# One exponential per head, and the check of the bounds put together at the end, in a top-k attention kernel

## The chip, the core and the metric

The kernel runs on one core of one Trainium2 chip. A core has five engines that each work through a queue of their own in order: TensorE (PE in the profile; PEld is its weight load), VectorE (DVE), ScalarE (ACT), GpSimd (POOL) and SyncE (SP), which here only starts transfers. They wait for one another through semaphores. The metric is the time of one execution in microseconds on the device: 827.2 us before the change, the median of three runs (826.03 to 827.62).

## What is computed

The reference is attention that keeps the 32 largest scores of each row, and behind it a mixture-of-depths block:

```python
# q, k, v: (8 batches, 8 heads, 576 tokens, 64), float32
scores = scale * np.matmul(q, k.transpose(0, 1, 3, 2))
kth = np.partition(scores, -top_k, axis=-1)[..., -top_k:-top_k + 1]   # top_k = 32
scores = np.where(scores >= kth, scores, -1000000000.0)
attn = np.exp(scores - max)            # max over each row
attn = attn / (sum of attn + 1e-09)
x = np.matmul(attn, v)                 # then (8, 576, 512), the heads side by side
# per batch b:
s = x[b] @ w_gate                      # 576 numbers
top_idx = the 128 tokens with the largest s
h = np.maximum(x[b, top_idx] @ w1, 0)  # w1: 512 x 1024
out[b, top_idx] = x[b, top_idx] + sigmoid(s)[:, None] * (h @ w2)
```

## The kernel before, in words

**Units.** The work is cut into 144 units `(b, t, g)`, 18 to a batch: a block of 128 query rows (the last block of a batch has 64, so it holds four heads instead of two) by two heads. A unit has two score tiles of 128 x 576, index `i` = 0 and 1; below they are called its two heads.

**What a unit goes through.** `multiply` computes the scores in PSUM and `keep` copies them out on ACT (`sc`). `find_bound` on DVE finds a lower bound of the 32nd largest score from the eight largest of each of seven parts. `what_is_below` marks on ACT which scores lie under the bound (`sides`) and counts them into `seen`, and on POOL forms `y`; `kth_of` on DVE takes the exact 32nd largest from `y` into `next8`. `mask_of` writes `less`, a 0/1 mask or a positive distance of what is too small, for one head on ACT and for the other on POOL. `weigh` transposes the scores on PE into `ptr` with, after each transposed block, a matmul that adds a hugely negative number where `less` is set (`turn`), does the same for the remaining 64 + 64 columns of both heads in the bank of `av` (`turn_last`), and then applies the exponential on ACT: one ACTIVATE over both heads, 1024 numbers in each partition, into `pT`, and one for `last`. `values` multiplies `pT` and `last` by v, `keep_values` copies the result to `xs`, and once per four units DVE and POOL normalise it.

**The order.** The loop at L1094 issues, in iteration n, work of different units: the exponential and the values of unit n-4, the mask of n-3, the 32nd largest of n-2, `what_is_below` of n-1, the bound of n, and the scores of n+1. All engines keep the order of the program (`InOrder`, L37), so this order is the order of each queue. Within an iteration, ACT has: exponentials of n-4 (L1124), mask of n-3, what the list `late` holds (`flush`, L1127), copies of transposed q and k, the copy of the scores (L1140), the copy of the values, then the two `sides`. PE has: the transposes and masks of n-4, the scores of n+1, the values of n-4, and a piece of the mixture of an earlier batch (its two matrix products are spread over the units of the next batch but one, at the places in `mix_at`).

**The check.** The shortcut through the bound is only right for ordinary inputs, so the kernel collects evidence and at the end decides whether to run a general version. For each batch, in the mask of its last unit (L1091), `keep_least` (L1073) takes the 36 bounds of each partition, tests with one bit operation on DVE whether a bound's mantissa is the wrong one (`low`), and reduces bounds, 32nd largest scores and `low` to one number each in `least`. For the last batch that is at L1255, in the tail. There the evidence is put together on DVE into `sure` (L1256 to L1278), and `count_unsure` multiplies `sure` by ones on PE (L1285).

**The tail.** After the loop, the last four units are finished in an order of their own (L1214 to L1252), `other_room` lending the scores' PSUM space to every second unit, and `closing` (L746) does the mixture of the last batch: gather of the chosen rows, four transposes, `xeT` copied by ACT, 64 matmuls with w1, 16 with w2, and the scatter. `closing` is a generator: what stands between two of its `yield`s goes into the queues between other work. The check stands at L1255 to L1281, after the step of `closing` that ends with `flush()` (L828), in which ACT gets `gy<-y_ps,g` of the batch before; and `count_unsure` stands ahead of the matmuls with w1 in PE's queue.

**PSUM.** It has eight banks: four for the scores (`ps`), two for `ptr`, one for `av`, one for the rest.

Of the kernel before, what the change touches and what calls it, by code (L numbers as in the profile page):

```python
# [26 lines left out]
LEAST = 1.0e-16 * SMALLER  # L27
# [4 lines left out]
J = 4  # L32
# [16 lines left out]
def kernel(  # L49
# [11 lines left out]
    nc = tc.nc  # L61
    P = nc.NUM_PARTITIONS
    B, H, S, D = q.shape
# [5 lines left out]
    R = S - JP  # L69
# [4 lines left out]
    scale = 1.0 / float(D) ** 0.5 / SMALLER  # L74
# [55 lines left out]

    NS = B * 2 * (J * NHP + NHP // 2)
    seen = const.tile([P, NS], FP32, name="seen")
    least = const.tile([P, 3, B], FP32, name="least")
    sums = const.tile([P, B * NT, H], FP32, name="sums")
    nc.gpsimd.memset(sums, 1.0)

# [50 lines left out]
    def flush():  # L187
        while late:
            late.pop(0)()
# [119 lines left out]
                    )  # L309

    def turn_pair(rows, hp, copy=None):
        tr = ps_tr.tile([P, 2, J, P], FP32, name="ptr")
        for w in range(2):
            rows.turn(2 * hp + w, tr[:, w, :, :])
        for w in range(2):
            rows.keep(2 * hp + w, tr[:, w, :, :], copy=copy)

    def turn_all_last(rows, copy=None):
        tr = ps_misc.tile([P, 2, 2, P], FP32, name="tr", tag="misc")
# [149 lines left out]
    def turn_some(tr, z, less):  # L469

        pe.transpose(tr, z, ident)
        if less is not None:
            pe.matmul(
                tr, less, out_of_reach, start=False, stop=True, skip_group_check=True
            )

    def room_to_turn():
        return ps_tr.tile([P, 2, J, P], FP32, name="ptr"), ps_av.tile(
            [P, 512], FP32, name="av"
        )  # L480

    def turn(z, tr, less=None):

        for i in range(2):
            for c in range(J):
                at = slice(c * P + i * R, (c + 1) * P + i * R)
                turn_some(
                    tr[:, i, c, :], z[:, i, at], None if less is None else less[:, i, at]
                )

    def turn_last(z, av, less=None):
# [11 lines left out]
    def values(t, g, pT, last, av, vs):  # L503

        vt, vpair = vs
        for i, heads in enumerate(heads_of(t, g)):
            for c in range(J):
                for r in (0, R):
                    h = heads[-1 if r else 0][0]
                    pe.matmul(
                        av[r : r + R, i * DE : (i + 1) * DE],
                        pT[:, i, c, r : r + R],
                        vt[:, h, c, :],
                        start=(c == 0 and i == 0),  # L520
                        stop=False,
                        skip_group_check=True,
                    )
# [222 lines left out]
    def closing(b, pg, between):  # L746
# [7 lines left out]
        pick = modpool.tile([P, NT, CAP], BF16, name="pick")  # L754

        def spread(t0, t1):
            tr = ps_tr.tile([P, 2, J, P], FP32, name="ptr")
            n = R if t0 == J else P
            for t in range(t0, t1):
                pe.transpose(  # L760
                    tr[:, 0, t - t0, 0:n],
                    gate[0:n, t : t + 1].to_broadcast([n, P]),
                    ident[0:n, 0:n],
                )
            act.copy(
                out=gate_row[:, t0 * P : (t1 - 1) * P + n].rearrange(
                    "p (t i) -> p t i", i=n
                ),
                in_=tr[:, 0, 0 : t1 - t0, 0:n],
            )  # L770

        def count(t, among, rank):
# [59 lines left out]
        dve.reciprocal(out=g, in_=g)  # L832

        xeT = modpool.tile([P, NDC, CAP], FP32, name="xeT")
        ps = ps_tr.tile([P, 2, J, P], FP32, name="ptr")[:, 0, :, :]
        for dc in range(NDC):
            pe.transpose(ps[:, dc, :], xe[:, dc * P : (dc + 1) * P], ident)
        act.copy(out=xeT, in_=ps)
# [2 lines left out]
        for f0 in range(0, NFC, 2):  # L841
            h_ps = (
                lambda: room_for_scores()[:, 0, 0, :],
                lambda: ps_av.tile([P, 512], FP32, name="av"),
                lambda: ps_misc.tile([P, 512], FP32, name="h_ps", tag="misc"),
                lambda: ps_tr.tile([P, 2, J, P], FP32, name="ptr")[:, 0, :, :].rearrange(
                    "p c i -> p (c i)"
                ),
            )[f0 // 2 % 4]()
# [186 lines left out]
    def weigh(sc, tr, av, less):  # L1036

        turn(sc, tr, less)
        tr_last = turn_last(sc, av, less)
        pT = ptpool.tile([P, 2, J, P], FP32, name="pT")  # L1040
        last = ptpool.tile([P, P], FP32, name="last")

        def exp():
            act.activation(pT, tr, AF.Exp, scale=scale)
            act.activation(last, tr_last, AF.Exp, scale=scale)

        return pT, last, exp
# [23 lines left out]
        find_kth(ys.pop(n), next8s[b][:, i, :, :])  # L1071

    def keep_least(b, bound, kth):  # L1073
        low = stats.tile([P, per_batch, 2], I32, name="low", bufs=1)
        dve.tensor_scalar(
            out=low,
            in0=bound.bitcast(I32),
            scalar1=(1 << 23) - 1,
            scalar2=1,
            op0=ALU.bitwise_and,  # L1080
            op1=ALU.bitwise_xor,
        )
        for w, of in enumerate((bound, kth, low)):
            dve.tensor_reduce(
                out=least[:, w, b : b + 1], in_=of, axis=mybir.AxisListType.XY, op=ALU.min
            )

    def mask_of(n, on=None):
        b, i = divmod(n, per_batch)
# [97 lines left out]

    def other_room():
        ps = room_for_scores()
        return ps[:, 0, :, :].rearrange("p u (c i) -> p u c i", c=J), ps[:, 1, 0, :]  # L1190

    x, pg = of_batch[B - 1]
    between = mixtures[B - 2]
# [59 lines left out]


    keep_least(B - 1, bounds.pop(B - 1)[:, :, :, 7], next8s.pop(B - 1)[:, :, :, 7])  # L1255
    sure = stats.tile([P, 1], FP32, name="sure")  # L1256
    dve.memset(sure, 1.0)
    for what, op, than, limit in (
        (least[:, 0, :], ALU.min, ALU.is_gt, LEAST),
        (least[:, 1, :], ALU.min, ALU.is_gt, LEAST),  # L1260
        (least[:, 2, :], ALU.min, ALU.is_gt, 0.5),
        (seen, ALU.max, ALU.is_lt, float(MIDDLE)),
        (seen, ALU.min, ALU.is_gt, float(MIDDLE - 16)),
        (sums.rearrange("p t h -> p (t h)"), ALU.min, ALU.is_gt, FEWEST),
        (sums.rearrange("p t h -> p (t h)"), ALU.max, ALU.is_lt, MOST),
    ):
# [62 lines left out]
    def general(b, row0):  # L1329
        def of(a):  # L1330
            return a[bass.ds(b, 1)].rearrange("o a s d -> (o a) s d")

        kT, qT, vs = room_for_qkv(0)
        rows = Rows(of(k), of(q), kT, qT)
        turn_all_last(rows)
        for hp in range(NHP):
            turn_pair(rows, hp)
        load_v(of(v), vs)
        x = xpool.tile([P, NT, HD], FP32, name="x")
        pg = gates_of[0]  # L1340
        for t in range(NT):
            xs = xpool.tile([P, H, DE], FP32, name="xs")
            for g in range(groups(t)):
                ps = room_for_scores()
                multiply(t, g, kT, qT, ps)
                p = general_weights(keep(ps))
                tr, av = room_to_turn()
                turn(p, tr)
                pT = ptpool.tile([P, 2, J, P], FP32, name="pT")
                last = ptpool.tile([P, P], FP32, name="last")  # L1350
                nc.scalar.copy(out=pT, in_=tr)
# [12 lines left out]
        flush_all()  # L1364
# [40 lines left out]
```

## Time and profile before

The profile is of one execution of its own:

| | before |
|---|---|
| median of three runs | 827.2 us |
| the profiled execution, as timed | 828.44 us |
| its span, first to last instruction | 826.1 us |
| its mean granted TensorE clock | 0.990 |
| busy: DVE, PE | 787.2 us, 777.0 us |
| busy: ACT, POOL | 730.7 us, 715.4 us |

So 2.3 us of the profiled execution lie outside its span, and it is 1.2 us over the median. In the lines of a profile, `out<-in` gives the tiles that an instruction writes and reads, `x` the number of instructions that a line stands for, and a bracket the idle time ahead of it and what ended that. Nearly all instructions are recorded under L45, the helper that issues them in order, so they are told apart by their tiles.

### The profile page before, as it was taken

What the parts mean: (1) busy time and instruction counts of PE and PEld (TensorE: products, weight loads), DVE (VectorE), ACT (ScalarE), POOL (GpSimd) and SP (SyncE); (2) the same over time, 40 slices, a digit from 0 to 9 for tenths busy, and PEclk for the clock granted to TensorE, in tenths of its full rate; (3) what the DMA queues carried; (4) which work ended last, traced back from release to release, by engine and by line L of the source; (5) the groups of instructions that cost most, each with busy time, mean ns of one, the idle gap of its engine ahead of it and who ended that gap; (6) DMA issues with size and microseconds to landing.
All of it is one profiled execution on the core that took longest, in us unless ns stands there. A gap on an engine that the chain in (4) does not pass through costs nothing. (4 is left out here: it accounts for less than half of the span.)

```text
span 826.1 us, 28252 instructions
## 1 busy us (share of the span) xinstructions
PE 777.0 (94%) x10143; PEld 596.5 (72%) x10143; DVE 787.2 (95%) x4651; ACT 730.7 (88%) x1557; POOL 715.4 (87%) x722
## 2 busy tenths in 40 slices
PE   6888888888999999999999999999999999999976
PEld 5566666666887778877787777877787777767744
DVE  7899999999999999999999999999999999999960
ACT  4799999999999999999999999999999999879831
POOL 3799999999899999999899999999999998899831
PEclk9699999999999999999999999999999999999999
DMA  7931111521141221521223221512215102101021
GB/s 170 283 86 40 28 66 28 105 53 27 60 92 36 53 40 59 112 47 34 79 47 86 53 40 60 104 23 54 40 59 112 28 15 66 23 12 18 2 71 30
DMA packets 122133, 50.38 MB, mean 61 GB/s; under 512 B 116417, under 2 KB 116417, under 8 KB 120961
## 3 DMA queue, kind: packets, MB, share of 16 engines
q1 hardware_dynamic: 118672, 43.91, 22.0%
q0 software_dynamic: 1728, 4.20, 2.8%
q8 instruction: 82, 1.34, 0.8%
q14 instruction: 67, 0.54, 0.3%
q10 hardware_dynamic: 1584, 0.39, 0.2%
HBM read 36.93 MB, written 11.55 MB: 59 GB/s over the span
## 5 line engine op out<-in xcount | busy, mean ns | idle before, releaser
L45 POOL TENSOR_TENSOR y<-sc,sides 128x576 f32<-128x576 f32 x288 | 365.1, 1289 | 57.0 <-ACT sides L45 54.3
L45 DVE MAX8 cand<-sc 128x8 f32<-128x82 f32 (+1 forms) x2016 | 314.0, 228 | 2.7 <-ACT sc L45 2.7
L45 POOL TENSOR_SCALAR less<-sc,next 128x576 bf16<-128x576 f32 x135 | 232.5, 1722 | 12.9 <-DVE next L45 10.0
L45 PE MATMUL ptr<-out_of_reach,less 128*128 128x128 bf16 x1136 | 205.3, 220 | 19.5 <-POOL less L45 19.4
L45 ACT ACTIVATE sides<-sc,bound 128x576 bf16<-128x576 f32 x288 | 223.0, 787 | 0.0
L45 PE MATMUL ptr<-ident,sc 128*128 128x128 f32 x1136 | 217.0, 282 | 0.0
L45 DVE MAX8 next<-y 128x8 f32<-128x584 f32 x288 | 204.4, 751 | 1.7 <-POOL y L45 1.6
L45 PEld LDWEIGHTS av<-v,pT 128*64 128x64 f32 x4544 | 144.1, 137 | 66.9 <-ACT last L45 63.2
L45 PE MATMUL ps<-kT,qT 64*128 64x288 f32 (+1 forms) x1280 | 182.0, 431 | 5.2 <-ACT qT L45 5.2
L45 PEld LDWEIGHTS ptr<-ident,sc 128*128 128x128 f32 x1136 | 161.3, 142 | 29.1 <-issue 17.4
L45 ACT ACTIVATE pT<-ptr 128x1024 f32<-128x1024 f32 x142 | 145.3, 1023 | 33.2 <-PE ptr L45 32.2
L45 PE MATMUL av<-v,pT 128*64 128x65 f32 x4544 | 163.7, 224 | 9.3 <-ACT last L45 8.5
L45 ACT COPY sc<-ps 128x1152 f32<-128x1152 f32 (+1 forms) x144 | 162.2, 1126 | 3.5 <-PE ps L45 3.5
L45 PEld LDWEIGHTS <-less 128*128 128x128 bf16 x1296 | 136.1, 106 | 39.2 <-POOL less L45 25.2
L45 PEld LDWEIGHTS ps<-kT,qT 64*128 64x128 f32 (+1 forms) x1280 | 100.2, 178 | 41.5 <-issue 21.2
L45 ACT ACTIVATE less<-sc,next 128x576 bf16<-128x576 f32 x143 | 111.2, 777 | 12.7 <-DVE next L45 10.8
L45 DVE MATCH_REPLACE8 cand<-best,cand 128x21 f32<-128x21 f32 (+1 forms) x576 | 99.0, 180 | 0.0
L45 DVE MAX8 best<-cand 128x8 f32<-128x21 f32 (+1 forms) x576 | 90.5, 190 | 0.0
L45 PE MATMUL h_ps<-xeT,w 128*128 128x128 f32 x464 | 65.8, 286 | 0.0
L45 PEld LDWEIGHTS h_ps<-xeT,w 128*128 128x128 f32 x464 | 55.8, 191 | 9.2 <-issue 5.8
L45 PE MATMUL y_ps<-w,hT 128*128 128x512 f32 x112 | 60.6, 636 | 0.0
L45 ACT ACTIVATION_READ_ACCUMULATOR sides<-sc,bound 128x1 f32 x288 | 59.9, 208 | 0.0
(133 smaller groups left out, 866.4 us busy)
## 6 DMA issues: line engine op xcount, KB each, us to landing
v<-in_v_dram SPq DMA_DIRECT2D x64, 128.0 KB, 4.2
out_dram<-x SPq DMA_DIRECT2D x8, 1024.0 KB, 3.9
rows<-in_k_dram SPq DMA_DIRECT2D x56, 128.0 KB, 2.9
rows<-in_q_dram SPq DMA_DIRECT2D x56, 128.0 KB, 3.1
w<-in_moe_w_dram SPq DMA_DIRECT2D x2, 2048.0 KB
gate_row<-row_dram SPq DMA_DIRECT2D x7, 288.0 KB, 4.4
w<-in_k_dram SPq DMA_DIRECT2D x8, 128.0 KB, 3.2
last<-in_k_dram SPq DMA_DIRECT2D x8, 128.0 KB, 4.0
```

The costliest lines, as they stand in the source:

```text
L45: return lambda *a, **kw: self._tc.keep_in_program_order(fn(*a, **kw))
```

## The change

The exponential becomes one ACTIVATE for each head, and each head gets its own PSUM bank (`ptr0`, `ptr1`) and its own SBUF tile (`pT0`, `pT1`) instead of half of a common one; the users of `ptr` elsewhere follow. `keep_least` no longer tests and reduces the bounds of a batch on DVE: ACT copies them, through the list `late`, into `bounded`, which holds those of all batches, 288 in each partition. The bit test and the reductions of `bounded` and `low` are done once, in the check at the end. The reduction of the 32nd largest scores stays in each batch.

```diff
-    least = const.tile([P, 3, B], FP32, name="least")
+    least = const.tile([P, B], FP32, name="least")
+    bounded = const.tile([P, NS], FP32, name="bounded")
...
     def turn_pair(rows, hp, copy=None):
-        tr = ps_tr.tile([P, 2, J, P], FP32, name="ptr")
+        tr = [turn_bank(w) for w in range(2)]
         for w in range(2):
-            rows.turn(2 * hp + w, tr[:, w, :, :])
+            rows.turn(2 * hp + w, tr[w])
         for w in range(2):
-            rows.keep(2 * hp + w, tr[:, w, :, :], copy=copy)
+            rows.keep(2 * hp + w, tr[w], copy=copy)
...
+    def turn_bank(i=0):
+        return ps_tr.tile([P, J, P], FP32, name=f"ptr{i}")
+
     def room_to_turn():
-        return ps_tr.tile([P, 2, J, P], FP32, name="ptr"), ps_av.tile(
-            [P, 512], FP32, name="av"
+        return [turn_bank(i) for i in range(2)], ps_av.tile([P, 512], FP32, name="av")
+
+    def room_for_weights():
+        return [ptpool.tile([P, J, P], FP32, name=f"pT{i}") for i in range(2)], ptpool.tile(
+            [P, P], FP32, name="last"
         )
...
         tr_last = turn_last(sc, av, less)
-        pT = ptpool.tile([P, 2, J, P], FP32, name="pT")
-        last = ptpool.tile([P, P], FP32, name="last")
+        pT, last = room_for_weights()
 
         def exp():
-            act.activation(pT, tr, AF.Exp, scale=scale)
+            for i in range(2):
+                act.activation(pT[i], tr[i], AF.Exp, scale=scale)
             act.activation(last, tr_last, AF.Exp, scale=scale)
...
     def keep_least(b, bound, kth):
-        low = stats.tile([P, per_batch, 2], I32, name="low", bufs=1)
-        dve.tensor_scalar(
-            out=low,
-            in0=bound.bitcast(I32),
-            scalar1=(1 << 23) - 1,
-            scalar2=1,
-            op0=ALU.bitwise_and,
-            op1=ALU.bitwise_xor,
-        )
-        for w, of in enumerate((bound, kth, low)):
-            dve.tensor_reduce(
-                out=least[:, w, b : b + 1], in_=of, axis=mybir.AxisListType.XY, op=ALU.min
-            )
+        at = 2 * per_batch * b
+        late.append(
+            lambda: act.copy(
+                out=bounded[:, at : at + 2 * per_batch].rearrange("p (n i) -> p n i", i=2),
+                in_=bound,
+            )
+        )
+        dve.tensor_reduce(
+            out=least[:, b : b + 1], in_=kth, axis=mybir.AxisListType.XY, op=ALU.min
+        )
...
     keep_least(B - 1, bounds.pop(B - 1)[:, :, :, 7], next8s.pop(B - 1)[:, :, :, 7])
+    flush()
+    low = modpool.tile([P, S], I32, name="low", tag="scratch")[:, 0:NS]
+    dve.tensor_scalar(
+        out=low,
+        in0=bounded.bitcast(I32),
+        scalar1=(1 << 23) - 1,
+        scalar2=1,
+        op0=ALU.bitwise_and,
+        op1=ALU.bitwise_xor,
+    )
     sure = stats.tile([P, 1], FP32, name="sure")
     dve.memset(sure, 1.0)
     for what, op, than, limit in (
-        (least[:, 0, :], ALU.min, ALU.is_gt, LEAST),
-        (least[:, 1, :], ALU.min, ALU.is_gt, LEAST),
-        (least[:, 2, :], ALU.min, ALU.is_gt, 0.5),
+        (bounded, ALU.min, ALU.is_gt, LEAST),
+        (least, ALU.min, ALU.is_gt, LEAST),
+        (low, ALU.min, ALU.is_gt, 0.5),
```

Left out of the diff are places that only follow the new tiles: `turn`, `values`, `spread`, `other_room`, the two uses of `ptr` in `closing`, and the general version, which does not run here.

More of the change, by code (lines that the diff above doesn't have):

```diff
@@ L487, in turn @@
                 turn_some(
-                    tr[:, i, c, :], z[:, i, at], None if less is None else less[:, i, at]
+                    tr[i][:, c, :], z[:, i, at], None if less is None else less[:, i, at]
                 )
@@ L517, in values @@
                         av[r : r + R, i * DE : (i + 1) * DE],
-                        pT[:, i, c, r : r + R],
+                        pT[i][:, c, r : r + R],
                         vt[:, h, c, :],
@@ L756, in spread @@
         def spread(t0, t1):
-            tr = ps_tr.tile([P, 2, J, P], FP32, name="ptr")
+            tr = turn_bank()
             n = R if t0 == J else P
@@ L760, in spread @@
                 pe.transpose(
-                    tr[:, 0, t - t0, 0:n],
+                    tr[:, t - t0, 0:n],
                     gate[0:n, t : t + 1].to_broadcast([n, P]),
@@ L768, in spread @@
                 ),
-                in_=tr[:, 0, 0 : t1 - t0, 0:n],
+                in_=tr[:, 0 : t1 - t0, 0:n],
             )
@@ L834, in closing @@
         xeT = modpool.tile([P, NDC, CAP], FP32, name="xeT")
-        ps = ps_tr.tile([P, 2, J, P], FP32, name="ptr")[:, 0, :, :]
+        ps = turn_bank()
         for dc in range(NDC):
@@ L845, in closing @@
                 lambda: ps_misc.tile([P, 512], FP32, name="h_ps", tag="misc"),
-                lambda: ps_tr.tile([P, 2, J, P], FP32, name="ptr")[:, 0, :, :].rearrange(
-                    "p c i -> p (c i)"
-                ),
+                lambda: turn_bank().rearrange("p c i -> p (c i)"),
             )[f0 // 2 % 4]()
@@ L1189, in other_room @@
         ps = room_for_scores()
-        return ps[:, 0, :, :].rearrange("p u (c i) -> p u c i", c=J), ps[:, 1, 0, :]
+        banks = [ps[:, 0, i, :].rearrange("p (c i) -> p c i", c=J) for i in range(2)]
+        return banks, ps[:, 1, 0, :]
     x, pg = of_batch[B - 1]
@@ L1348, in general @@
                 turn(p, tr)
-                pT = ptpool.tile([P, 2, J, P], FP32, name="pT")
-                last = ptpool.tile([P, P], FP32, name="last")
-                nc.scalar.copy(out=pT, in_=tr)
+                pT, last = room_for_weights()
+                for i in range(2):
+                    nc.scalar.copy(out=pT[i], in_=tr[i])
                 nc.scalar.copy(out=last, in_=turn_last(p, av))
```

## The prediction

> **What bounds the kernel now.** I read the page's busy times first, then the busy times by stretches of one batch, then the instructions in order of time around the removed work and in the tail. The chain of work that ended last was no help: it follows back only the final scatter.
>
> ```profile
> span 826.1 us, 28252 instructions
> PE 777.0 (94%) x10143; PEld 596.5 (72%) x10143; DVE 787.2 (95%) x4651; ACT 730.7 (88%) x1557; POOL 715.4 (87%) x722
> ```
>
> DVE leads and PE is close behind. Cut at the places where `low` runs, which are one batch apart:
>
> ```profile
> core 0: us, PE busy (x) PEld busy (x) DVE busy (x) ACT busy (x) POOL busy (x), PEclk, DMA share, GB/s
> 209.70:306.10 96.40, 95.06 (x1263) 73.60 (x1261) 96.22 (x577) 91.83 (x198) 88.81 (x88) 1.00 0.27 60
> 306.10:402.20 96.10, 94.93 (x1261) 73.58 (x1261) 95.99 (x577) 91.53 (x198) 88.51 (x88) 1.00 0.27 60
> 594.50:690.60 96.10, 95.37 (x1265) 74.20 (x1265) 95.99 (x578) 91.55 (x197) 88.47 (x88) 1.00 0.22 49
> 690.60:780.00 89.40, 86.66 (x1137) 67.94 (x1136) 87.33 (x520) 75.66 (x159) 80.71 (x80) 1.00 0.10 25
> ```
>
> In the middle of the kernel DVE idles about 0.1 us per batch: DVE sets the pace there, and an instruction taken off DVE is time gained, until the next engine is full. That is PE, with 1.34, 1.17 and 0.73 us idle in the first three rows. ACT has some 4.5 us per batch.
>
> **The change part by part: DVE in the loop.** This is what `keep_least` costs now:
>
> ```profile
> 402.23 1.06 DVE L45 TENSOR_SCALAR low<-bound 128x36 int32<-128x36 int32 x1
> 403.20 0.21 DVE L45 TENSOR_REDUCE least<-bound 128x1 f32<-128x36 f32 x1
> 403.34 0.20 DVE L45 TENSOR_REDUCE least<-next 128x1 f32<-128x36 f32 x1
> 403.46 0.17 DVE L45 TENSOR_REDUCE least<-low 128x1 f32<-128x36 int32 x1
> 403.56 1.10 DVE L45 MAX8 cand<-sc 128x8 f32<-128x82 f32 x7
> ```
>
> Records of one engine overlap, so the price is from start to start: 1.33 us for the four, of which the reduction from `next` (0.12) stays: 1.21 us saved. `low` takes 1.06 us because POOL runs `y<-sc,sides` up to that moment; with POOL idle in the tail the same instruction takes 0.18 us. The seven batches in the loop give 0.32 (the first, where `low` took 0.17 us), 1.39, 1.22, 1.21, 1.22, 1.22 and 1.16, together 7.74 us. PE caps this: per batch I take the smaller of the saving and PE's idle time (1.34, 1.17, 1.16, 1.27, 0.73 from the second saving on; 2.74 in the last row; in the first batch PE idles 12 us). 0.32 + 1.34 + 1.17 + 1.16 + 1.22 + 0.73 + 1.16 = **7.1 us gained**. Bounds: 7.7 if PE's idle time is no limit, 3.5 if half of it is waits that stay.
>
> **The exponential on ACT.** Two instructions of 512 replace one of 1024, 144 times. No exponential of 512 is in the trace; the nearest rows are ACT's copies and scalings of 128x512 out of the same `ptr`.
>
> ```profile
> 20.23 0.57 ACT L45 COPY kT<-ptr 128x512 f32<-128x512 f32 x1
> 20.70 0.60 ACT L45 ACTIVATE qT<-ptr 128x512 f32<-128x512 f32 x1
> ...
> 390.67 1.02 ACT L45 ACTIVATE pT<-ptr 128x1024 f32<-128x1024 f32 x1 [0.38 <-PE ptr L45]
> 391.59 0.27 ACT L45 ACTIVATE last<-av 128x128 f32<-128x128 f32 x1
> ```
>
> By durations the second instruction costs 0.57 + 0.60 - 1.02 = 0.15 us, 22 us in all. From start to start it is 0.47 for a 512 and 0.92 for the 1024, so 0.02 to 0.05 us, at most 7 us in all. I take 0.05, since starts decide what a queue can pass; 0.9 us per batch out of ACT's 4.5 us is covered. At 0.15, 2.7 us per batch is still under 4.5, but not in every stretch (see the rivals).
>
> [...]
>
> Against this cost: ACT waits for PE before `pT`.
>
> ```profile
> ACT pT L45 <- PE ptr L45: 32.2, 75, 1.6
> ```
>
> These waits (0.43 us on average) end when both heads are transposed. The first head is complete 4 x 0.17 = 0.68 us earlier, and in the changed kernel's queues each of the two instructions has its own wait for PE. So in such a unit `last` starts up to 0.44 us earlier (0.92 - 0.48). It doesn't shorten DVE's work, so I count it at nothing in the loop; it is what lets PE use its idle time, since PE's values wait for `last`. The values still start after `last`: their first matmul carries one wait for all three exponentials, as before.
>
> **ACT's copies of the bounds.** Seven in the loop, 36 elements each, nearest row `found<-av` (128x6, 0.17 us, 0.06 from start to start) and `sums<-xs` (0.22 us): 0.06 to 0.2 us, behind the mask and ahead of the score copy. DVE uses that copy an iteration later (copied by 404.55, used from 408.37), so 3.8 us of slack cover it: nothing, 1.4 us if the cover is gone. No DMA is moved, and SP and POOL issue what they issued.
>
> **Start and tail of the exponential.** At the start `kT<-ptr` (11.81, after 0.37 us of waiting) can begin before the second transposed tile; its followers up to DVE's wait of 1.50 us at 25.39 inherit it: 0 to 0.45 gained, taken 0.3, because that chain has no other wait in it but the half-speed clock of that stretch. After the loop, `pT` at 780.29 has waited 1.61 us for PE; `sides`, `y` and the last 32nd-largest search (DVE waited 1.35 us for it) follow: 0 to 0.44 gained, taken 0.3.
>
> **The check in the tail.** This is the loss. These are ACT, DVE and PE around it:
>
> ```profile
> 804.23 0.69 ACT L45 ACTIVATE gy<-y_ps,g 128x512 f32<-128x512 f32 x1 [2.98 <-PE y_ps L45]
> 805.52 0.59 ACT L45 COPY xeT<-ptr 128x512 f32<-128x512 f32 x1 [0.60 <-PE ptr L45]
> ...
> 802.18 0.45 DVE L45 TENSOR_REDUCE far<-seen 128x1 f32<-128x288 f32 x1
> 804.96 0.16 DVE L45 TENSOR_TENSOR sure<-sure,far 128x1 f32<-128x1 f32 x1
> ...
> 805.41 0.19 PE L45 MATMUL av<-ones,sure 128*1 128x1 f32 x2
> 806.16 2.05 PE L45 MATMUL ps<-xeT,w 128*128 128x128 f32 x16 [0.56 <-ACT xeT L45]
> ```
>
> Today the check runs on DVE from 800.93 to 805.12 beside the gather and hides. The new copy of the last batch's bounds stands in ACT's queue behind `gy<-y_ps,g`, which waits for PE until 804.23 and ends at 804.92; the copy ends near 805.05. DVE's `low` now waits for it, and behind `low` on DVE stand the whole check and the two small steps on `g`. `low` over 288: between 0.10 us (the 36-element row, start to start) and 0.53 (`less`, 128x576); taken 0.30, for its size lies halfway. Then `bounded` (a reduction of 288 and its product take 0.56 start to start, by the `seen` rows), `least` 0.27, `low` 0.56: 805.08 + 0.30 + 1.39 = 806.77. The rest is as before, 805.12 - 802.18 = 2.94: `sure` is there at 809.71. PE's count waits for it, and in PE's queue the w1 products stand behind the count; they start near 809.90 instead of 806.16. All that follows to the end is one chain (w1, `hT`, w2, `gy`, scatter): **3.7 us lost**, 3.5 to 4.0 by the bounds of `low`, 5.2 if POOL's scatter at 805.52 holds `low` up as POOL does in the loop.
>
> **Sum.** -7.1 - 0.3 - 0.3 + 3.7 = -4.0 us: the profiled execution's 828.44 becomes 824.4. It lay 1.2 above the median, so on the median 827.2 becomes about 823.3; I say 823.5.
>
> **Rivals.**
> - *PE keeps its waits.* Half of PE's idle time stays, loop -3.5: net -0.4, time 826.8. For it: in the second row 1.0 of the 1.17 us is PE waiting for `last`, which ACT may still deliver late. Against: 11 of 18 exponentials per batch wait for PE and now start earlier.
> - *ACT becomes the bound where it is full (slower).* From 391 to 322 us of the next batch, about five units, ACT is busy 5.2 to 5.3 of 5.34 us. At 0.15 to 0.18 us per split plus the copy, some 1.1 us per batch is added there and none can be hidden if DVE's slack is used up: 6 x 1.1 = 6.6 eats the loop's 7.1, and the tail's 3.7 remains: net about +2.6, time 829.8. It decides from some 0.12 us per split. Against: the start-to-start rows, and 3.6 us of slack between ACT and DVE.
> - *The tail hides it.* If the count did not hold PE up: -7.7, time 819.5. Against: the queue order on ACT, DVE and PE.
> - *The split starts nothing earlier.* Excluded by the separate waits; it would give back 0.6 us.
>
> **How the numbers follow.** The forecast (net -2 to -5.2, 822 to 825.2) has 0.55, PE's waits 0.20, ACT the bound 0.18, a hidden tail 0.07. A change of 0.2% (1.65 us) is about what can be told from none. Faster 0.62, same 0.20, slower 0.18. `prod` on DVE varies between 0.67 and 1.2 us with POOL's phase, five per batch, which may move the loop by 2 us either way. The range goes from 820.5 to 829: it holds the forecast with this, PE's waits and part of the slower case.
>
> **What would show it.** Right: `low` and two of three `least` reductions gone from the loop, batches of about 95 us, DVE with small waits and PE with none; `low<-bounded` waiting for ACT some 4 us near the end and `av<-ones,sure` 4 us later against the gather. Wrong: batches of 96 us or more with ACT at 95 us; or w1 products that start right after `xeT`.

## The result and the profile after

The changed kernel is slower: 831.4 us, median of six runs (829.35 to 833.02), against 826.7 us for the kernel before (825.6 to 827.62, six runs on the same chip). The ratio is 1.0055, 95% interval 1.0041 to 1.0069. The prediction said 823.5 us and faster. The profiled execution took 831.12 us with a span of 828.8, so its own excess over the profiled execution before is 2.7 us; that one lay 1.8 above the median of the six.

The page's busy times of the changed kernel:

```profile
span 828.8 us, 28383 instructions
PE 777.0 (94%) x10143; PEld 596.2 (72%) x10143; DVE 786.2 (95%) x4628; ACT 743.6 (90%) x1709; POOL 721.6 (87%) x722
```

23 instructions are gone from DVE, among them six `low` of 1.0 to 1.2 us, and yet DVE's busy time fell by only 1.0 us, from 787.2. POOL executes the same 722 instructions and needs 6.2 us more. ACT has 13 us more: its exponentials into `pT` alone go from 145.3 to 160.3 us. The busy times by stretches of the changed kernel, cut where DVE searches the last unit of a batch (span, then each engine's busy time and count, clock, DMA share, GB/s):

```profile
core 0: us, PE busy (x) PEld busy (x) DVE busy (x) ACT busy (x) POOL busy (x), PEclk, DMA share, GB/s
207.85:303.97 96.12, 94.86 (x1263) 73.40 (x1261) 95.91 (x574) 93.33 (x216) 89.36 (x88) 1.00 0.27 60
303.97:400.11 96.14, 94.77 (x1261) 73.43 (x1261) 96.00 (x574) 93.37 (x216) 89.39 (x88) 1.00 0.27 60
400.11:496.24 96.13, 94.75 (x1261) 73.41 (x1261) 95.99 (x574) 93.35 (x216) 89.36 (x88) 1.00 0.27 60
```

A batch takes 96.13 us, where it took 96.11 before and 95 was forecast, and DVE still shows hardly any idle time, 0.14 to 0.21 us. Three DVE instructions fewer in each batch (577 to 574), the same time, no idle time to speak of: other instructions must have become longer. PE's idle time didn't shrink either; it is 1.26 to 1.38 us.

From here on "a batch" is the time from the start of the search (`next<-y`) for a batch's last unit to the same point of the next, for batches 3 to 5 of 0 to 7, where nothing of the start or the end reaches. Where the changed kernel stands against the kernel before, in the two profiles:

| stretch | before | after | gained (+) or lost (-) by the end of it |
|---|---|---|---|
| search of unit 0 | 22.45 | 21.96 | +0.5 |
| search of unit 1 | 28.92 | 27.05 | +1.9 |
| last unit of batch 5 | 593.12 | 591.04 | +2.1 |
| last unit of batch 6 | 689.22 | 688.19 | +1.0 |
| last unit of batch 7 | 785.33 | 782.06 | +3.3 |
| `row_i` (the gather can start) | 800.80 | 797.57 | +3.2 |
| last `gy` on DVE | 820.55 | 823.00 | -2.5 |

So the loop, which was to bring 7.1 us, brought about nothing until its last batch; the start and the last batch brought more than forecast; and the tail lost 5.7 us, not 3.7. The loss of 1.0 in batch 6 (97.15 us) is not the change's doing for certain: e3 and e4 below have the same loop and 96.27 and 96.14 there, while e9 and e12 have it again.

**Where the 1.2 us of a batch went.** Instructions of DVE and POOL in order of time around units 5 and 6 of a batch, the kernel before:

```profile
338.85 1.71 POOL L45 TENSOR_SCALAR less<-sc,next 128x576 bf16<-128x576 f32 x1
339.72 0.29 DVE L45 TENSOR_SCALAR pick<-slot,ranks 128x128 bf16<-128x128 f32 x1
344.28 1.72 POOL L45 TENSOR_SCALAR less<-sc,next 128x576 bf16<-128x576 f32 x1
344.67 0.89 DVE L45 CUSTOM_DVE_ANT_0 prod<-x,wg 128x512 f32<-128x512 f32 x1
```

and the same units in the changed kernel:

```profile
336.69 1.72 POOL L45 TENSOR_SCALAR less<-sc,next 128x576 bf16<-128x576 f32 x1
336.79 0.72 DVE L45 TENSOR_SCALAR pick<-slot,ranks 128x128 bf16<-128x128 f32 x1
342.06 1.71 POOL L45 TENSOR_SCALAR less<-sc,next 128x576 bf16<-128x576 f32 x1
342.17 1.17 DVE L45 CUSTOM_DVE_ANT_0 prod<-x,wg 128x512 f32<-128x512 f32 x1
```

`prod` begins 0.39 us behind the start of POOL's `less` before and 0.11 behind it after, and ends 1.28 us behind it both times. DVE came 0.28 us earlier and its instruction took 0.28 us longer. The same holds all through both traces: from 100 to 690 us, every `prod` of 128x512 that begins 0.11 to 0.47 us behind the start of a `less` ends 1.27 to 1.30 us behind it (17 in the kernel before, 14 in the changed one), and one that begins 0.62 us behind or later, or just ahead, takes 0.67 to 0.73. A `pick` that begins in the first 0.2 us ends 0.81 or 0.82 behind. DVE passes the border of the batch some 1.1 us earlier relative to POOL; then `prod` at unit 0 takes 0.24 more (it now meets the end of POOL's `y`), `pick` at unit 5 0.43, `prod` at unit 6 0.28, `prod` at unit 14 0.12 and the `prod` over 64 rows 0.05, together 1.1: the saving is gone before the next border. None of it shows as idle time (0.14 to 0.21 us a batch), because DVE's record covers the time in which it is held: 1.17 us for the `prod` above, 0.67 for a free one.

The groups by form say the same in sums, in the kernel before:

```profile
L45 DVE CUSTOM_DVE_ANT_0 prod<-x,wg 128x512 f32<-128x512 f32 x32 | 29.9, 934 | 1.4 <-POOL x L45 1.4
L45 DVE TENSOR_SCALAR pick<-slot,ranks 128x128 bf16<-128x128 f32 x7 | 2.4, 340 | 0.3
```

and in the changed one:

```profile
L45 DVE CUSTOM_DVE_ANT_0 prod<-x,wg 128x512 f32<-128x512 f32 x32 | 32.3, 1009 | 1.5 <-POOL x L45 1.4
L45 DVE TENSOR_SCALAR pick<-slot,ranks 128x128 bf16<-128x128 f32 x7 | 4.7, 677 | 0.3
```

**The tail.** ACT, DVE and PE around the check in the changed kernel, in order of time:

```profile
801.01 0.69 ACT L45 ACTIVATE gy<-y_ps,g 128x512 f32<-128x512 f32 x1 [2.98 <-PE y_ps L45]
801.59 0.25 ACT L45 COPY bounded<-bound 128x36 f32<-128x36 f32 x1
801.87 0.31 DVE L45 TENSOR_SCALAR low<-bounded 128x288 int32<-128x288 int32 x1 [3.96 <-ACT bounded L45]
...
806.57 0.19 PE L45 MATMUL av<-ones,sure 128*1 128x1 f32 x2 [4.30 <-DVE g L45]
806.69 3.78 PE L45 MATMUL ps<-xeT,w 128*128 128x128 f32 x16
```

The wait is the one that was forecast: `low` stands 3.96 us behind ACT's copy, the count on PE 4.30 us behind DVE, and the products with w1 start 5.05 us after the gather's transposes (801.64) instead of 1.30: 3.75 lost. What was not forecast is the 3.78 us of the first 16 products, which took 2.05 before. The same stretch by windows:

```profile
806.60:808.00 1.40, 1.40 (x8) 1.37 (x9) 0.24 (x2) 0.00 (x0) 0.00 (x0) 0.50 0.04 6
808.00:810.30 2.30, 2.30 (x13) 2.30 (x13) 0.00 (x0) 0.00 (x0) 0.00 (x0) 0.50 0.01 4
```

The granted clock is 0.50 from PE's first product (806.57) up to 810.85 us, and it was 0.50 already from 804.10 on, while PE stood still; in the kernel before it was 1.00 there. By the products of the second bank 2.0 us are lost to it (3.58 and 2.08 us from start to start, where it was 1.89 and 1.79).

### The profile page after: what moved, and what is told of

It reads as the page before. It is cut to its first block, busy times and chain, and to the rows that moved or that the text cites. A ratio compares the mean times of both kernels' runs of the same rounds, so it can differ in the third digit from the quotient of the medians.

```text
span 828.8 us, 28383 instructions
## 1 busy us (share of the span) xinstructions
PE 777.0 (94%) x10143; PEld 596.2 (72%) x10143; DVE 786.2 (95%) x4628; ACT 743.6 (90%) x1709; POOL 721.6 (87%) x722
## 3 DMA queue, kind: packets, MB, share of 16 engines
q1 hardware_dynamic: 118672, 43.91, 22.4%
## 5 line engine op out<-in xcount | busy, mean ns | idle before, releaser
L45 PEld LDWEIGHTS ptr<-ident,sc 128*128 128x128 f32 x1136 | 160.6, 141 | 29.4 <-issue 17.4
L45 ACT ACTIVATE pT<-ptr 128x512 f32<-128x512 f32 x284 | 160.3, 598 | 9.9 <-PE ptr L45 5.2
L45 PEld LDWEIGHTS <-less 128*128 128x128 bf16 x1296 | 135.0, 105 | 37.6 <-POOL less L45 23.9
```

Source lines behind the costliest of these rows:

```text
L45: return lambda *a, **kw: self._tc.keep_in_program_order(fn(*a, **kw))
```

## The experiments

Each ratio is to runs of the kernel before on the same chip. e7 and e10 leave work out, so their times are no times of the whole computation.

| run | time, us | ratio [95%] | a batch, us |
|---|---|---|---|
| after | 831.4 | 1.0055 [1.0041, 1.0069] | 96.13 |
| e1 | 824.5 | 0.9983 [0.9971, 0.9995] | 96.19 |
| e2 | 831.7 | 1.0068 [1.0049, 1.0087] | 95.98 |
| e3 | 824.0 | 0.9976 [0.9966, 0.9985] | 96.13 |
| e4 | 828.1 | 1.0027 [1.0014, 1.0040] | 96.14 |
| e5 | 826.3 | 1.0002 [0.9988, 1.0016] | 96.30 |
| e6 | 840.9 | 1.0188 [1.0158, 1.0217] | 98.45 |
| e7 | 823.8 | 0.9979 [0.9967, 0.9991] | 96.04 |
| e8 | 826.2 | 1.0009 [0.9998, 1.0021] | 96.30 |
| e9 | 825.2 | 0.9976 [0.9961, 0.9991] | 96.13 |
| e10 | 819.1 | 0.9916 [0.9891, 0.9941] | 95.69 |
| e11 | 826.8 | 0.9998 [0.9988, 1.0009] | 96.57 |
| e12 | 824.8 | 0.9982 [0.9970, 0.9995] | 95.90 |
| e13 | 822.5 | 0.9957 [0.9940, 0.9973] | 95.70 |
| e14 | 824.8 | 0.9978 [0.9965, 0.9991] | 95.97 |
| e15 | 824.0 | 0.9962 [0.9944, 0.9980] | 96.47 |
| e16 | 824.1 | 0.9967 [0.9955, 0.9978] | 95.77 |

### e1 and e2: each half of the change alone

e1 is the changed kernel with the check of the kernel before; e2 is the kernel before with the check of the changed one.

```diff
 # e1, from after: keep_least and the check as before
+        low = stats.tile([P, per_batch, 2], I32, name="low", bufs=1)
+        dve.tensor_scalar(out=low, in0=bound.bitcast(I32), ...)
+        for w, of in enumerate((bound, kth, low)):
+            dve.tensor_reduce(out=least[:, w, b : b + 1], in_=of, ...)
 # e2, from before: keep_least and the check as after
+        late.append(lambda: act.copy(out=bounded[...], in_=bound))
+        dve.tensor_reduce(out=least[:, b : b + 1], in_=kth, ...)
```

> Only the split of the exponential (own banks, own tiles); the check is that of the kernel before. Theory A (in the loop PE and ACT set the pace, some 96.1 us per batch, and what is taken off DVE only lets POOL hold other DVE instructions for longer): batches of 96.1 us although DVE has the 1.2 us back, low near 1.06 us again, the early start kept (1.7 us at the first batch border), the tail as before; about 823.5 us against 826.7. Theory B (DVE sets the pace, and the saving was lost to longer prod and pick by chance of phase): the batches of the changed kernel plus 1.2 us, 97.3 us; about 830 us.

> Only the check is put together at the end, with ACT's copies of the bounds; one exponential over both heads. Theory A: batches stay at 96.1 us, the start is that of the kernel before, the tail loses 3.7 us to the wait and some 2 us to the slower clock after it: about 832 us. Theory B: 1.2 us off each batch, tail +5.7: about 825.5 us.

The split alone gains 0.17%, the check alone loses 0.68%; together they make the 0.55% of the whole within the intervals. The split doesn't slow a batch beyond 0.08 us. The check alone saves about 0.13 us per batch of the 1.2 that it takes off DVE, so it was not the split that ate the saving. Its trace has the lost time partly in another place: `pick` costs 0.35 us more per batch than in the kernel before, and the one `less` of a batch that DVE writes, which now runs beside POOL's `y`, 0.72. This `less` in e2:

```profile
390.93 1.21 DVE L45 TENSOR_SCALAR less<-sc,next 128x576 bf16<-128x576 f32 x1
```

and in the changed kernel, where it takes what it took before:

```profile
391.23 0.50 DVE L45 TENSOR_SCALAR less<-sc,next 128x576 bf16<-128x576 f32 x1
```

Its tail (from `row_i` to the last `gy`) is 26.2 us, as in the changed kernel (25.4) and not as before (19.75).

### e3 and e4: the tail

e3 lets ACT copy the last batch's bounds earlier, ahead of `gy<-y_ps,g` in its queue. e4 leaves the wait where it is and gives PE 34 small products (128x128) ahead of the count, whose result nobody reads.

```diff
 # e3, from after
+    keep_least(B - 1, bounds.pop(B - 1)[:, :, :, 7], next8s.pop(B - 1)[:, :, :, 7])
+    flush()
     ...                                    # a step of closing that gives ACT gy<-y_ps,g
-    keep_least(B - 1, bounds.pop(B - 1)[:, :, :, 7], next8s.pop(B - 1)[:, :, :, 7])
-    flush()
 # e4, from after, in count_unsure
+        for _ in range(34):
+            pe.matmul(ps[:, P : 2 * P], out_of_reach, out_of_reach)
```

> The changed kernel with the last batch's copy of the bounds (and its reduction on DVE) put before the second step of closing, so that it stands in ACT's queue ahead of gy. If the copy behind gy is the whole cause in the tail: DVE's low does not wait, the w1 products start 1.3 us after the gather's transposes as before, at full clock, and the time is 5.7 us under the changed kernel, about 824 to 825 us. If the longer check itself (288 instead of 8 numbers) costs the tail: some 3 us stay, about 828 us.

> The changed kernel with 34 bf16 matmuls of constants on PE ahead of the count, where PE waits 4.3 us for sure. If the slow w1 products behind that wait (3.58 us where it was 1.89, then 2.08 where it was 1.79) come from the clock after idling: they take 1.9 and 1.8 us, the wait itself stays, and the time falls by 2 us against the changed kernel, to about 829.4 us. If not: no change beyond 0.3 us.

In e3 the tail is 19.7 us again, and the kernel is 0.24% faster than the one before. That is no more, within the intervals, than the 0.17% of the split alone (e1), whose batches take as long (96.19 and 96.13): what the check takes off DVE in the loop can't be told from nothing. The chain of e3 in order of time: `low` waits for nothing, the count 0.18 us, the products 0.31 us.

```profile
796.61 0.30 DVE L45 TENSOR_SCALAR low<-bounded 128x288 int32<-128x288 int32 x1
...
801.31 0.19 PE L45 MATMUL av<-ones,sure 128*1 128x1 f32 x2 [0.18 <-DVE g L45]
801.80 2.05 PE L45 MATMUL ps<-xeT,w 128*128 128x128 f32 x16 [0.31 <-ACT xeT L45]
```

In e4 the wait stays and the slow clock goes:

```profile
801.47 0.31 DVE L45 TENSOR_SCALAR low<-bounded 128x288 int32<-128x288 int32 x1 [3.96 <-ACT bounded L45]
801.61 2.06 PE L45 MATMUL av<-out_of_reach 128*128 128x128 bf16 x34
...
806.08 0.19 PE L45 MATMUL av<-ones,sure 128*1 128x1 f32 x2 [2.41 <-DVE g L45]
806.20 2.05 PE L45 MATMUL ps<-xeT,w 128*128 128x128 f32 x16
```

PE still idles 2.41 us, but not 4.30, and the products take 2.05 us. The tail is 23.3 us: of 5.7 us lost, 2.1 were the clock and 3.6 the wait. The first products behind 4.30 us of idleness ran at a granted clock of 0.50, those behind 2.41 us at 1.00. The length of one stand-still does not settle it, though: in e7 below the clock is 0.50 from 795.25 to 801.90 us, and PE stood still for no longer than 2.38 us at a time in the tail ahead of it.

### e5 to e10: what sets the 96.1 us

All six start from e3. e5 and e6 add two and five reductions of `wg` (0.68 us each) to DVE at the border of a batch; e7 leaves out half of the 16 products with w2 of each batch in the loop, 4.2 us of PE; e8 moves the copy `xeT` of the loop from ACT to DVE; e9 moves the one `pick` of each batch that is DVE's to POOL; e10 lets `prod` go over 64 of the 512 columns.

```diff
 # e5 (2) and e6 (5), in keep_least
+            for _ in range(2):
+                dve.tensor_reduce(out=idle, in_=wg, axis=mybir.AxisListType.X, op=ALU.min)
 # e7, in the mixture of the loop
+            if fc % 2 == 0:
+                pe.matmul(ps, hT[:, fc, :], w2[:, fc, :], start=(fc == 0), stop=(fc == NFC - 2))
 # e8
-        late.append(lambda ps=ps: act.copy(out=xeT, ...))
+        vector_late.append(lambda ps=ps: dve.tensor_copy(out=xeT, ...))
 # e9
-                if t == 0:
+                if exact and t == 0:
                     choose_slot(dve, t, n)
 # e10
-            out=prod[0:n, 0:HD], in0=x, in1=wg[0:n, :],
+            out=prod[0:n, 0:64], in0=x[:, 0:64], in1=wg[0:n, 0:64],
```

The letters of the theories are explained where the expectations first use them.

> The kernel with the early copy, and at each batch border in the loop two extra reductions of 512 constants on DVE (near 0.65 us each, 1.3 us per batch), whose result nothing uses. Theory A (PE and ACT set the pace; DVE has some 2.2 us per batch in which prod and pick only take longer beside POOL): batches stay within 0.2 us of 96.13, and prod and pick get shorter. Theory B (DVE sets the pace): 97.4 us per batch, 8 us in all.

> As the run with two extra reductions, but five of them, near 3.3 us per batch, more than the 2.2 us. Theory A: about 1 us per batch comes through, batches near 97.2 us. Theory B: 99.4 us per batch.

> The kernel with the early copy and half of the second product of the mixture left out in the loop (every second matmul of y_ps, 4 x 1.06 us of PE per batch, so what is added to the chosen rows is not the reference's). Theory A: PE's dense units get shorter until ACT or DVE fills them, batches of 94.5 to 95.5 us. Theory B: 96.1 us as before.

> The kernel with the early copy, and the loop's copy xeT (0.46 us from start to start) moved from ACT to DVE, where it costs some 0.65 us. At the batch border ACT is full and PE waits for last. Theory A: batches 0 to 0.5 us shorter, 95.6 to 96.1 us. Theory B: 0.65 us longer, 96.8 us.

> The kernel with the early copy, and the one pick per batch that DVE forms (0.29 us alone, 0.6 to 0.7 us where it now meets POOL's less) given to POOL with the other four. Theory C (DVE does set the pace, its holds by POOL counted in; the saving was handed back as longer prod and pick, since POOL did not come earlier by the same 1.1 us): the 0.7 us are DVE's, so batches fall by 0.3 to 0.7 us, to 95.4 to 95.8 us, less what the next prod takes back. Theory A (some other engine sets 96.1): no change beyond 0.1 us.

> The kernel with the early copy, and the product for the gate on DVE taken over 64 of the 512 columns (the rest is left out, so other rows are chosen and the output is not the reference's): each of the five prod per batch loses about 0.5 us of work and meets less of POOL's work. Theory C: 2 to 3.5 us off each batch on DVE, of which PE (94.4 us of work) lets some 1.2 to 2 us through, batches of 94 to 95 us. Theory A: 96.1 us.

*PE is not the pace.* With 4.2 us less of PE's work a batch is 0.09 us shorter. PE's busy time in 96 us falls from 94.6 in e3 to 92.3, and DVE's and POOL's stay:

```profile
305.00:401.00 96.00, 92.31 (x1255) 71.90 (x1253) 95.86 (x574) 92.60 (x216) 89.34 (x88) 1.00 0.27 60
```

*DVE's holds are a spring.* 1.36 us more on DVE (e5) make a batch 0.17 us longer; 3.4 us (e6) make it 2.3 longer. That is between what the two theories expected of e6 (97.2 and 99.4). Some 1.1 to 1.2 us of what is added does not come through, most of it taken out of the holds: in e5 `prod` over 128 rows needs 29.2 us where e3 has 32.5, over 64 rows 8.4 for 10.2, and `pick` 2.9 for 4.2, together 0.9 us per batch. What is taken away goes into them: in e9 `pick` is gone and unit 5 is 0.74 us shorter, but `prod` grows to 36.8 us and a batch stays at 96.13. In e10, whose `prod` does an eighth of the work, it still takes 755 ns in the mean:

```profile
L45 DVE CUSTOM_DVE_ANT_0 prod<-x,wg 128x64 f32<-128x64 f32 x32 | 24.2, 755 | 1.5 <-POOL x L45 1.4
```

where the one that was least disturbed takes 0.21 us. A batch falls by 0.44 us. So theory A fits e5 and e9 and fails in e7, theory B fits e7 and fails in e5, and in e10 neither A's 96.1 nor C's 94 to 95 us comes out. e8 says less: DVE's copy made PE wait for it, so the move has a second effect.

### e11 and e12: ACT at two places of the batch

From e3, three extra copies of `wg` (0.60 to 0.73 us each) on ACT, in the iterations of units 1 to 3 (e11) or 9 to 11 (e12).

```diff
+        if n >= per_batch and n % per_batch in (3, 4, 5):        # e12: (11, 12, 13)
+            act.copy(out=idle, in_=wg)
         if is_unit(n):
             bound_of(n)
```

> The kernel of e3 with three extra copies of wg (128x512, SBUF to SBUF) on ACT in each batch but the first, one each in the iterations in which DVE does the 32nd largest of units 1, 2 and 3; nothing else changes. The nearest row, xeT<-xe_ps 128x512, takes 0.58 us and 0.46 from start to start, so about 1.4 us of ACT work per batch. Theory C (ACT sets the pace between the last unit of a batch and unit 6 of the next, where in e3 it never waits and delivers its mask 0.1 to 0.8 us after DVE's value could have released it; DVE only follows): what is added there comes through, batches of 97.2 to 97.6 us instead of 96.13, time about 832 to 834. Theory D (DVE with its holds beside POOL sets the pace; ACT is 2 to 4 us ahead of what DVE needs): batches of 96.1 to 96.4, time 824 to 826.

> As e11, with the three copies in the iterations in which DVE does the 32nd largest of units 9, 10 and 11, where ACT waits for DVE before its mask (0.2 to 0.3 us per unit in e3). Theory C: ACT has slack to DVE there; of 1.4 us about half is taken by ACT's waits in units 9 to 15 and the rest by its lead over DVE, so batches of 96.1 to 96.5, time 824 to 827, clearly less than e11. Theory D: the same as e11, 96.1 to 96.4. If ACT sets the pace everywhere, both take the full 1.4 us per batch: 97.5, about 833.

Neither theory holds. At the border some 1.6 us of ACT's work (0.52 from start to start for each) cost 0.44 us, a third of what theory C expected and more than theory D allows. In the middle the added work made a batch *shorter*, by 0.23 us on average. The trace shows what moved: ACT is later there, POOL's `less` with it, and `prod` now comes just ahead of it. DVE and POOL in e12:

```profile
362.31 0.72 DVE L45 CUSTOM_DVE_ANT_0 prod<-x,wg 128x512 f32<-128x512 f32 x1
362.47 2.15 POOL L45 TENSOR_SCALAR less<-sc,next 128x576 bf16<-128x576 f32 x1
```

`prod` is free of the hold, and `less` takes 2.15 us instead of 1.72: the one that came second was held, here as in the lines before. In all, `prod` takes 29.4 us in e12 and 32.5 in e3, three microseconds saved on DVE by making ACT slower. Over the whole kernel nothing is gained by it (824.8 us, 824.0 in e3): batch 6 takes 97.16 us, and the last batch 94.87, where e3 has 96.27 and 93.68.

### e13 and e14: DVE's queue moved past the hold

What DVE does between the two halves of the bound (the normalising, `prod`, the picks) is put four maxima later in its queue, 0.63 us; in e13 from e3, in e14 from the kernel before.

```diff
-            if i == 1:
-                flush_vector()
             for u in range(PARTS):
+                if i == 1 and u == 4:
+                    flush_vector()
                 dve.max(
```

> The kernel of e3, in which what DVE does between the two halves of the bound (the normalising, prod, the picks) stands four of the 128x82 maxima later in DVE's queue, about 0.63 us; same work. In after and e3, prod that begins 0.1 to 0.63 us behind the start of POOL's less always ends 1.28 us behind it, and prod that begins ahead of it or 0.63 us or more behind it takes 0.67 us; at 0.63 us later most should begin outside this stretch. Theory H (the 1.2 us taken off DVE came back as these holds, and DVE with its holds sets the pace): prod 128x512 falls from 32.5 us in all to 22 to 25, batches from 96.13 to 95.0 to 95.7, time 818 to 822. Theory P (POOL and ACT set the pace and the holds are only the place where DVE waits for them): prod is short, but batches stay at 96.0 to 96.2, time 823 to 825, and DVE shows the time as idle or in another instruction.

> The kernel before with the same shift of DVE's queue and nothing else of the change. Its prod is held less (29.9 us in all, where 21.5 would be free) and its pick not at all. Theory H: batches of 95.3 to 95.9 instead of 96.11, time 822 to 825, and e13's batches shorter than these by most of the 1.2 us that the change takes off DVE. Theory P: batches as before, 96.0 to 96.2, time 826 to 828, and no shorter in e13 than here.

e13 takes 95.70 us a batch and 822.5 us in all, faster than both kernels by more than the interval; e14 takes 95.97. The saving is then worth 0.27 us a batch where it was worth -0.02, between the theories. But there was less to save in e14: at its new place `low` takes 0.42 us instead of 1.06, 0.35 from start to start, so the three instructions cost 0.58 us there, and about half of that came through. `prod` did not become short: 30.7 us in e13, still above what the kernel before has. At 0.63 us later some of them begin ahead of `less`, but DVE as a whole moved up against POOL and met the next `less` in its first 0.4 us: of the 24 over 128 rows from 100 to 690 us, 12 still end 1.28 to 1.30 us behind its start. The holds formed again.

### e15 and e16: what holds e13 at 95.70

The ACT work of e11 and e12 on top of e13.

> The kernel of e13 with the three extra ACT casts of wg (0.65 to 0.67 us recorded each, about 1.6 us per batch from start to start) in the iterations of units 1 to 3. In e13 ACT's mask begins 0.2 to 1.4 us behind what DVE would allow in units 17 to 6. Theory Q (95.70 is the pace of ACT and POOL there): batches 96.9 to 97.4, time 831 to 834. Theory R (95.70 is still DVE with its holds, and ACT has slack as in e11, where 1.6 us gave 0.45): 95.9 to 96.3, time 824 to 827.

> As e15 with the casts in the iterations of units 9 to 11, where in e13 ACT's mask is within 0.05 to 0.45 us of DVE's value. Theory Q, if ACT's queue is full all through the batch: 96.7 to 97.3, time 829 to 833. Theory R: 95.4 to 96.0, time 820 to 825, as e12 moved the kernel of e3 by -0.3 us per batch.

At the border 0.77 us of some 1.6 come through, in the middle 0.07. Theory R holds in the middle and neither at the border. So even here ACT has slack over most of a batch, and about half of what is added counts between the last unit of a batch and unit 6 of the next, where in e3 it waits for nobody. No single engine was found whose work sets the time of a batch: PE's doesn't, ACT's counts by a quarter to a half in one stretch of it, DVE's by an eighth in small amounts and two thirds in large ones. That POOL and ACT together set the places against which DVE is held is argued from the positions; no run varied POOL's own work alone, and what the floor of 95.7 consists of stays open.

## Why the prediction was wrong, step by step

- **"DVE sets the pace there, and an instruction taken off DVE is time gained, until the next engine is full"**: this step failed. It was read from DVE's idle time of 0.1 us per batch. But some of DVE's busy time is time in which POOL holds it (up to 0.5 us of a `prod`, 1.17 recorded for 0.67), and this part gives: of the 7.1 us put down for the loop, 5.9 were to come up to the last unit of batch 6, and between unit 1 and there the two profiles show -0.8 (0.0 with e3's 96.27 us for batch 6 in place of 97.15). The cap by PE's idle time, which the prediction was careful about, was beside the point, as e7 showed. The prediction did see that `low` takes 1.06 us beside POOL and 0.18 alone, and that `prod` varies between 0.67 and 1.2 with POOL's phase; it made a margin of 2 us either way of it, and did not ask whether the saving itself would move that phase: in the changed kernel DVE comes 0.28 us earlier to the same `less` and is held 0.28 us longer. The sign isn't fixed, for in e2, e12 and e13 some `prod` get ahead of `less` and run free; and why a batch stays near 96.1 us all the same is open.
- **The exponential on ACT**: right in its size. In the changed kernel a pair starts 0.96 us ahead of `last`, where one of 1024 took 0.92:

```profile
399.17 1.05 ACT L45 ACTIVATE pT<-ptr 128x512 f32<-128x512 f32 x2
400.13 0.27 ACT L45 ACTIVATE last<-av 128x128 f32<-128x128 f32 x1
```

  The price is 0.04 us from start to start, as taken, although the busy time rose by 13 us; e1 shows no loss. ACT's waits for PE went as described, from 32.2 us in 75 waits to 5.2 us in 9; the waits of the changed kernel (sum, number, longest):

```profile
ACT pT L45 <- PE ptr L45: 5.2, 9, 0.9
PEld av L45 <- ACT last L45: 39.0, 66, 1.3
```

- **The start**: 0.3 us were taken, 1.9 came. The step up to unit 0 agrees in this pair of profiles (0.5, at the upper bound of 0.45), though this time varies by 1.1 us among the 15 profiles with the split (21.39 to 22.52). Beyond it, the products of the next scores, which ran at the slow clock before, met the fast one. In order of time, the kernel before:

```profile
21.36 2.29 PE L45 MATMUL ps<-kT,qT 64*128 64x288 f32 x8 [2.03 <-ACT qT L45]
```

  and after:

```profile
20.53 1.24 PE L45 MATMUL ps<-kT,qT 64*128 64x288 f32 x8 [2.03 <-ACT qT L45]
```

  DVE's wait of 1.50 us for those scores is gone. The windows show a mean granted clock of 0.88 from 20.0 to 21.3 us and 0.50 from 21.4 to 23.6 before, and 1.00 up to 21.8 us and 0.75 from there to 23.0 after: PE came 0.83 us earlier, and the drop 1.4 us later. That the drop moved is not the change's doing. In e2, which has no split, these products meet the fast clock:

```profile
21.37 1.24 PE L45 MATMUL ps<-kT,qT 64*128 64x288 f32 x8 [2.04 <-ACT qT L45]
```

  and in e4, which has it, the slow one:

```profile
20.35 2.29 PE L45 MATMUL ps<-kT,qT 64*128 64x288 f32 x8 [2.03 <-ACT qT L45]
```

  With the split, the search of unit 1 starts anywhere between 26.65 and 28.38 us in these profiles, without it at 28.92, 27.88 (e2) and 27.36 (e14). So most of the 1.9 us was the luck of the two profiled executions. The prediction had the slow clock as given.
- **The last batch**: 1.16 + 0.3 were taken, 2.2 came. The border's 1.0 stayed a gain here. The rest is units 14 to 17, where the two profiles' distance grows from 2.06 to 3.27 us: 1.2, not 0.3. This is the split's doing: in the same units e1, the split alone, gains 1.2 on the kernel before (2.95 to 4.11), and e2, without it, nothing (3.26 to 3.30). There ACT waits for PE ahead of the exponentials of several units, and the prediction counted the earlier first half for one of them; that this is how the split gains it is argued, not tested.
- **The check in the tail**: mechanism, place and size of the wait were right (3.7 forecast, 3.75 in the trace, 3.6 by e4). The missing term is the clock after the wait, 2.0 us, which the prediction put at nothing without a word and which the trace of before could not show, since PE never idled for longer than 1.53 us in its tail.
- **The rivals**: "PE keeps its waits" fell with e7, and "ACT becomes the bound" with e1, where the split costs no more than 0.08 us a batch. The slower rival's loss was to come from the split; it came from a gain that stayed away and a tail that cost more. The margin for POOL's phase named the right place for the lost time, with the wrong weight.

Summed up in the profiles: start +1.9, from unit 1 to the last unit of batch 6 -0.8, last batch +2.2, tail -5.7: 2.5 us lost, to rounding, at the last `gy`, 2.7 in the timed execution. Between the medians the loss is 4.7 us, since the profiled execution of before lay 1.8 above its median and that of after 0.3 below. e3 and the changed kernel differ in nothing but the tail, and there by 5.7 us in the profiles; their ratios put 6.5 us between them, and the rest is not traced to anything.

## What to carry to other kernels

A busy engine without idle time need not set the pace: look first whether some of its instructions end at a fixed distance from another engine's, as `prod` did here, 1.27 to 1.30 us behind the start of POOL's `less`. The record hid a wait, and the 1.2 us taken off a batch came back as longer instructions. When a step in a tail is made to wait, ask how long TensorE then stands still (4.30 us here), and whether the first products behind it will run at a lower clock (0.50 here, which cost 2.0 us). And put a copy that a later check needs ahead of the waits in its queue: the same change with one copy moved (e3) was faster than the kernel before, and with DVE's work moved by four maxima (e13) its ratio was lower again, 0.9957 [0.9940, 0.9973] against 0.9976 [0.9966, 0.9985], at 822.5 us.

## What the runs showed of the hardware

- A `prod` on DVE (two inputs from SBUF, 0.67 us when it is free) that begins 0.08 to 0.58 us behind the start of POOL's `less` (1.72 us) ends 1.27 to 1.31 us behind it, whenever it began; one that begins between 0.17 us ahead and 0.06 us behind takes 0.67 to 0.74, and then `less` takes 2.15 to 2.26 us (all profiles but e10, from 100 to 690 us; at 0.07 us behind both are seen). So POOL's `less` held DVE for about 0.6 us (1.28 less 0.67), a third of its recorded time, and DVE's `prod`, where it came first, made `less` longer by 0.43 to 0.54.
- Work added to ACT made batches 3 to 5 shorter (e12, 96.13 to 95.90 us), and in them `prod` on DVE ran ahead of POOL's `less` instead of behind it; the whole kernel was no faster.
- In the tail PE took up its work at full clock after 2.41 us of idleness (e4), and after 4.30 us at 0.50, for some 4.3 us (the changed kernel; e2 the same after 4.35). In e7 the clock was 0.50 from 795.25 to 801.90 us behind waits of at most 2.38 us.
- At the start of the kernel the granted clock fell to 0.50 at another time in each profiled execution: 21.0 us in the kernel before, 22.4 in the changed one, near 20.0 in e4 and 23.9 in e2. It decided whether eight products took 1.24 or 2.29 us.
